# Moving rows of the MLP's output matrix onto 24 lanes, splitting its first products and single-buffering the staging tiles in a one-token attention and MLP kernel

## The chip, the cores and the metric

The kernel runs on one core of a Trainium2 chip. The metric is the device time of one execution in microseconds (us). The kernel before takes 662.61 us, the median of three runs that lie between 662.54 and 662.67.

## The reference, cut to what matters

For 4 sequences with one new token each, a normalised input feeds two branches, and the output is the input plus both.

```python
xn = _layernorm(x)                                   # x: 4 x 1 x 640
q = (xn @ wq).reshape(B, Sq, Hq, Dh)                 # 32 heads of 128
scores = einsum('bhqd,bhkd->bhqk', q, k) * Dh**-0.5  # k, v: 4 x 32 x 4096 x 128
o = einsum('bhqk,bhkd->bhqd', softmax(scores), v)
A = o.reshape(B, Sq, Hq * Dh) @ wo                   # wo: 4096 x 640

z = _gelu(xn @ w_in)                                 # w_in: 640 x 1728
z1, z2 = z[..., :864], _layernorm(z[..., 864:])
B = (z1 * (w_sp * z2 + b_sp)) @ w_out                # w_out: 864 x 640
out = x + A + B
```

The key and value caches are 134 MB each and are read once. All else that is read is about 14 MB.

## The kernel before, in words

A **unit** is one sequence and eight heads. There are 16 units (4 groups of heads, 4 sequences). A unit's keys, 8 MB, come as four quarters of 2 MB into a ring of seven places (`ring`), its values into `v_all`, 8 MB. A lane (one of 128 partitions) holds a run of 256 keys of one head.

For each quarter `n`, the loop from L688 issues `product(n)` (L504, VectorE multiplies the keys in place by the query), `fold_half(n)` (L510, VectorE adds the upper half of each key's products to the lower), `sums(n)` (L519, eight TensorE matmuls against an identity sum the rest) and, one step later, `row_sums(n)` (L532, VectorE). When a unit is complete, `head_max` and `exps` (L554, ScalarE) make the probabilities `p_c`, `by_head` (L565) spreads them to `p_m`, and `weighted` (L589, TensorE) multiplies them by the values. `take` (L601, ScalarE) copies the result to `o_rows`, `pick_unit` (L620) gathers the heads, and once per group `group_turn` and `group_proj` (L650) multiply by `wo`.

Nearly all transfers are issued on the SP queue, by `pump()`, in the order of the list `loads` (L179 to L187): half of unit 0's keys, the MLP's weights (`load_w`, L119), the other half, unit 1's keys, then values of unit u and keys of unit u+2 by turns, with `wo` after each fourth unit. A load is issued as soon as its place is free: keys when the sums that read the place are done, values when `weighted` is. Transfers in flight share eight completion semaphores, so the ninth transfer waits for the first, and so on. The instruction order on TensorE, VectorE, ScalarE and SP is the order of the program text (L684).

The MLP is the generator `gmlp()` (L362). Its parts are run between the steps of quarters 0 to 2, at the `next(mlp)` calls (L692, L701, L703, L720). The first part is the products with `w_in` (L370). The last is the products with `w_out` (L470) into the output accumulator `out_ps`. `w_in` and `w_out` lie in `v_all` until unit 0's values may be loaded.

The 864 rows of `w_out` are cut in two. Rows 0 to 767 lie on 128 lanes, six to a lane: five in `v_all` (`w_out_sb`), the sixth in `p_m` (`w_row_sb`). The last 96 rows lie on lanes 0 to 23, four to a lane, in `p_m` (`w_end_sb`). Those come by four transfers on ScalarE's queue (L117), each of six lanes (`l:FT:LS` takes every fourth lane).

At the end, the last columns of `wo` arrive in pieces, the last two of 80 KB each (L215), and the last matmuls of L650 wait for them. `out_ps` holds the two column halves of the output in lanes 0 to 3 and 32 to 35. VectorE copies the left half of these columns to `res` (L773), ScalarE the right half (L774), and two transfers write the output (L775, L776).

Of the kernel before, what the change touches and what calls it, by code (L numbers as in the profile page):

```python
# [9 lines left out]
FP32 = mybir.dt.float32  # L10
BF16 = mybir.dt.bfloat16
# [6 lines left out]
def kernel(  # L18
# [28 lines left out]
    QD = 32  # L47
# [6 lines left out]
    NR = HT * S // P  # L54
# [4 lines left out]
    RW = 8  # L59
    QW = HC * Dh  # L60
    RING = 2 * NK - 1
    NFF = Fh // P
    FR = 4
    FT = (Fh - NFF * P) // FR
    NFC = NFF + FR
    LS = 4
    NOH = D // 2
    CB = 4
    NG = NR // CB
    GW = CB * Dh  # L70
    JR = Dh // QD
# [5 lines left out]
    const = ctx.enter_context(tc.tile_pool(name="const", bufs=1))  # L77
    work = ctx.enter_context(tc.tile_pool(name="work", bufs=1))
    small = ctx.enter_context(tc.tile_pool(name="small", bufs=2))
    PSUM = bass.MemoryType.PSUM  # L80
    ps_s = ctx.enter_context(tc.tile_pool(name="ps_s", bufs=2, space=PSUM))
    ps_pv = ctx.enter_context(tc.tile_pool(name="ps_pv", bufs=2, space=PSUM))
# [12 lines left out]
    v_all = places.tile([P, NK * QW], BF16, name="v_all")  # L95
# [3 lines left out]
    w_in_sb = v_all[:, DC * HD : DC * (HD + F)].rearrange("p (c n) -> p c n", c=DC)  # L99


    NV = NFF - 1
    at_v = -(-DC * (HD + F) // 256) * 256
    w_out_sb = v_all[:, at_v : at_v + NV * D].rearrange("p (k n) -> p k n", k=NV)
    p_w = p_m[:].rearrange("p n g c h -> p (n g c h)")
    at_p = -(-D // 256) * 256
    w_row_sb = p_w[:, 0:D]
    w_end_sb = p_w[:, at_p : at_p + FR * D].rearrange("p (r n) -> p r n", r=FR)
    nc.sync.dma_start(out=wq_sb, in_=A_wq.rearrange("(p c) n -> p c n", c=DC))

    wsp_bf = const.tile([1, 1], BF16)
    bsp_bf = const.tile([1, 1], BF16)
    nc.scalar.dma_start(out=wsp_bf[:], in_=B_w_sp[0:1, 0:1])
    nc.scalar.dma_start(out=bsp_bf[:], in_=B_b_sp[0:1].rearrange("(a b) -> a b", a=1))
    w_end_rows = B_w_out[NFF * P : Fh].rearrange("(p r) n -> p r n", r=FR)
    for l in range(LS):
        nc.scalar.dma_start(out=w_end_sb[l:FT:LS], in_=w_end_rows[l:FT:LS])  # L117

    def load_w():  # L119
        nc.sync.dma_start(out=w_in_sb, in_=B_w_in.rearrange("(p c) n -> p c n", c=DC))  # L120
        w_rows = B_w_out[0 : NFF * P].rearrange("(p k) n -> p k n", k=NFF)
        nc.sync.dma_start(out=w_out_sb, in_=w_rows[:, 0:NV])
        nc.sync.dma_start(out=w_row_sb, in_=w_rows[:, NV])

    def run_of(cache, u):
        hg, b = divmod(u, Bsz)
# [122 lines left out]
    for i in range(NSTAT):  # L249
# [5 lines left out]
        out=rstd[:], in_=mv[:, 1:2], func=ACT.Sqrt, bias=eps_tile[:Bsz], scale=1.0  # L255
    )
    nc.vector.reciprocal(out=rstd[:], in_=rstd[:])
    xn_bf = work.tile([Bsz, D], BF16)
    nc.vector.tensor_scalar(
        out=xn_bf[:],  # L260
        in0=x_bf[:],
        scalar1=mv[:, 0:1],
        scalar2=rstd[:],
# [1 line left out]
        op1=ALU.mult,  # L265
    )

    xn_v = xn_bf[:].rearrange("b (p c) -> b c p", c=DC)
    xnT_ps = ps_m.tile([P, DC, Bsz], BF16, tag="m")
    for c in range(DC):  # L270
        nc.tensor.transpose(
# [2 lines left out]
    xnT = const.tile([P, DC, QD], BF16)  # L274
    nc.vector.memset(xnT[:], 0.0)
    nc.vector.tensor_copy(out=xnT[:, :, 0:Bsz], in_=xnT_ps[:])


    wq_v = wq_sb.rearrange("p c (g k e d) -> p c k e g d", g=HG, k=NQ, e=PAR)
# [59 lines left out]
    OG = 32  # L339
# [22 lines left out]
    def gmlp():  # L362
        zz, gw, gt, gz = (gm[n] for n in ("zz", "gw", "gt", "gz"))
        zT = ps_pv.tile([P, 2, NFC, Bsz], FP32, tag="pv", name="zT")
        for t in range(2):
            f1 = t * Fh + NFF * P
            w_t = w_in_sb[:, :, t * Fh : f1].rearrange("p c (f k) -> p c k f", k=NFF)
            for k in range(NFC):
                for c in range(DC):
                    nc.tensor.matmul(  # L370
                        out=zT[: P if k < NFF else FT, t, k, :],
                        lhsT=w_t[:, c, k, :]
                        if k < NFF
                        else w_in_sb[:, c, f1 + k - NFF : f1 + FT * FR : FR],
                        rhs=xnT[:, c, 0:Bsz],
                        start=(c == 0),
                        stop=(c == DC - 1),
                    )
        yield
        nc.vector.tensor_copy(out=zz[:, :, 0:NFF, :], in_=zT[:, :, 0:NFF, :])  # L380
        nc.vector.tensor_copy(out=zz[:FT, :, NFF:], in_=zT[:FT, :, NFF:])
        nc.vector.tensor_tensor(out=gw[:], in0=zz[:], in1=zz[:], op=ALU.mult)
        nc.vector.tensor_scalar(
            out=gw[:], in0=gw[:], scalar1=0.044715, scalar2=1.0, op0=ALU.mult, op1=ALU.add
# [77 lines left out]
            op=ALU.add,  # L462
        )
        nc.vector.tensor_tensor(out=gm["yT"][:], in0=gz[:, 0, :, :], in1=sq, op=ALU.mult)
        w_terms = [w_out_sb[:, k] for k in range(NV)] + [w_row_sb]
        w_terms += [w_end_sb[:FT, r] for r in range(FR)]
        for k in range(NFC):
            w = P if k < NFF else FT
            for half in range(2):
                nc.tensor.matmul(  # L470
                    out=out_sum(half),
                    lhsT=gm["yT"][:w, k, :],
                    rhs=w_terms[k][:, half * NOH : (half + 1) * NOH],
                    start=False,
                    stop=False,
                )
# [51 lines left out]
    def row_sums(n):  # L528
        u, r, t = step(n)
        if n % NK == 0:  # L530
            scores[u] = small.tile([P, NR], FP32, name="s_sb")
        nc.vector.tensor_reduce(  # L532
            out=scores[u][:, r * HC : (r + 1) * HC],
            in_=sums_ps.pop(n)[:],
            axis=AX.X,
            op=ALU.add,
        )
# [12 lines left out]

    def exps(u):
        hg, b = divmod(u, Bsz)
        p_c[u] = small.tile([P, NR], BF16, name="p_c")
        nc.scalar.activation(  # L554
            out=p_c[u][:],
            in_=scores.pop(u)[:],
            func=ACT.Exp,
            bias=maxes.pop(u)[:],
            scale=1.0,
            accum_out=row_den[hg % NACC][:, b : b + 1],  # L560
        )
# [35 lines left out]
    gr, taken, rdens = {}, {}, {}  # L597

    def take(u):
        o = taken[u] = small.tile([P, CB, Dh], FP32, name="o_rows")  # L600
        nc.scalar.copy(out=o[:].rearrange("p c d -> p (c d)"), in_=pvs.pop(u)[:])  # L601

    def group_den(hg):
# [24 lines left out]
    def group_turn(hg):  # L628
        rden = small.tile([P, 1], FP32, name="rden")
        nc.vector.reciprocal(out=rden[:], in_=rdens.pop(hg)[:])  # L630
        o_n = small.tile([P, JR, QD], BF16, name="o_n")
        nc.vector.tensor_scalar(
            out=o_n[:].rearrange("p j q -> p q j"),
            in0=gr.pop(hg)[:].rearrange("p (q j) -> p q j", j=JR),
            scalar1=rden[:, 0:1],
            scalar2=None,
            op0=ALU.mult,
        )
        o_t = small.tile([P, JR, QD], BF16, name="o_t")
        nc.vector.transpose(  # L640
            out=o_t[:].rearrange("p j q -> p (j q)"), in_=o_n[:].rearrange("p j q -> p (j q)")
        )
        gr[hg] = [
            o_t[:, j, Bsz * e : Bsz * (e + 1)] for e in range(PAR) for j in range(JR)
        ]
# [38 lines left out]
    with tc.manual_schedule(engines={E.PE, E.DVE, E.Activation, E.SP}):  # L684
# [3 lines left out]
        for n in range(NK * NU):  # L688
            u, i = divmod(n, NK)
            product(n)  # L690
            if n in (1, 2):
                next(mlp)  # L692
            if n:
                row_sums(n - 1)
            if i == 0 and u:
                head_max(u - 1)
                if waiting in taken:
                    picked(waiting)
            fold_half(n)
            if n == 1:  # L700
                next(mlp)  # L701
            if n in (1, 2):
                next(mlp)  # L703
            if i == 0 and u:
                exps(u - 1)
                if waiting in pvs:
                    take(waiting)
                by_head(u - 1)
            sums(n)
            if i == 0 and u + 1 < NU:  # L710
                stage_q(u + 1)
            if i == 0 and waiting is not None:
                if waiting in taken:
                    picked(waiting)
                if waiting % Bsz == Bsz - 1:
                    group_turn(waiting // Bsz)
                    group_proj(waiting // Bsz)
                waiting = None
            if n == 0:
                next(mlp)  # L720
            if n == 2:
                busy.remove(V)
            if n in turns:
# [45 lines left out]

        res = work.tile([P, NOH], BF16, name="res")  # L770
        out_v = out.flatten_outer_dims()
        mid = NOH // 2
        nc.vector.tensor_copy(out=res[0 : OG + Bsz, 0:mid], in_=out_ps[0 : OG + Bsz, 0:mid])  # L773
        nc.scalar.copy(out=res[0 : OG + Bsz, mid:NOH], in_=out_ps[0 : OG + Bsz, mid:NOH])  # L774
        nc.scalar.dma_start(out=out_v[:, 0:NOH], in_=res[0:Bsz])  # L775
        nc.sync.dma_start(out=out_v[:, NOH:D], in_=res[OG : OG + Bsz])  # L776

# [29 lines left out]
```

## Time and profile before

| | us |
|---|---|
| median of three runs | 662.61 |
| the profiled execution: its own time | 662.73 |
| the profiled execution: its span | 660.9 |
| VectorE busy in the span | 522.6 |
| TensorE matmul busy in the span | 311.6 |
| ScalarE busy in the span | 29.7 |

282.24 MB are read in the span, 427 GB/s. In the profile, DMA is the mean busy share of the core's 16 DMA engines. A line of the profile names the program line (L519), the engine (PE is TensorE, DVE is VectorE, ACT is ScalarE, SP is the queue that issues most transfers), and what is written and read.

The trace also holds every DMA packet: its start, duration, size and queue. It doesn't say which of the 16 DMA engines moved it. An engine moves one packet after another without a gap, so its next packet starts 3 to 6 ns before the end of the one before. That lets the packets be strung together, engine by engine, as long as no two engines are at the same point.

### The profile page before, as it was taken

The numbers are of one execution on the slowest core, as the hardware profiler recorded it, in microseconds if no ns is written. First come the engines' busy times: TensorE is split into PE (matmuls) and PEld (weight loads), VectorE is DVE, ScalarE is ACT, GpSimd is POOL, SyncE is SP. The second block draws the span as 40 slices with busy tenths as digits, with TensorE's granted clock in tenths as the row PEclk, the third lists the DMA queues.
The fourth block names the chain that finished last, engine by engine and source line by source line (L and its number), as shares of the span: only waits on it lengthen the run. The fifth ranks groups of instructions, "written<-read, shape, count | busy, mean of one in ns | idle before, by whom it ended". The sixth has DMA issues, their size and how long they took to land.

```text
span 660.9 us, 4698 instructions
## 1 busy us (share of the span) xinstructions
PE 311.6 (47%) x2035; PEld 135.9 (21%) x2035; DVE 522.6 (79%) x326; ACT 29.7 (4%) x73; POOL 2.7 (0%) x12
## 2 busy tenths in 40 slices
PE   0264363526437363462536347262452644637457
PEld 0131121212213121130222112121120221213124
DVE  2478988959597794969959597695959969999940
ACT  0020000000000000000000000000000000000000
POOL 1000000000000000000000000000000000000000
PEclk9756586766768676576767767676685767857685
DMA  9999999999999999999999999999999999999996
GB/s 374 429 449 436 418 444 440 429 440 425 436 432 437 424 437 432 440 433 424 429 445 437 424 432 433 436 433 440 428 433 432 433 436 432 414 436 428 449 412 269
DMA packets 8497, 282.56 MB, mean 428 GB/s; under 512 B 888, under 2 KB 2180, under 8 KB 3356
## 3 DMA queue, kind: packets, MB, share of 16 engines
q1 hardware_dynamic: 8408, 282.12, 99.0%
q8 instruction: 16, 0.26, 0.1%
q10 hardware_dynamic: 68, 0.13, 0.1%
q14 instruction: 5, 0.04, 0.0%
HBM read 282.24 MB, written 0.01 MB: 427 GB/s over the span
## 4 chain that ended last, share of the span: by engine, by line
DMA 60%; DVE 29%; PE 10%; issue 1%; DVEq 0%; ACT 0%
DMA k_ring<-in_A_k_cache_dram 52%; DVE k_ring L504 15%; DVE k_ring L510 8%; PE s_ps L519 7%; DMA v_all<-in_A_v_cache_dram 4%; DMA k_ring<-in_A_wo_dram 3%; DVE s_sb L532 2%; DVE p_m L565 1%; DVE m L541 1%; PE out_ps L650 1%; PE pv L589 1%; PE zT L370 1%; DVE mt L543 0%; PE out_ps L470 0%; DVE mt L546 0%
## 5 line engine op out<-in xcount | busy, mean ns | idle before, releaser
L504 DVE TENSOR_TENSOR k_ring<-k_ring,qbc 128x8192 bf16<-128x8192 bf16 x64 | 282.8, 4418 | 87.7 <-DMA k_ring<-in_A_k_cache_dram 87.7
L519 PE MATMUL s_ps<-k_ring,ident 128*128 128x512 bf16 x512 | 200.5, 562 | 313.1 <-DVE k_ring L510 313.1
L519 PEld LDWEIGHTS <-ident 128*128 128x128 bf16 x512 | 65.2, 129 | 427.1 <-issue 382.6
L510 DVE TENSOR_TENSOR k_ring<-k_ring 128x4096 bf16<-128x4096 bf16 x64 | 146.0, 2282 | 0.0
L589 PE MATMUL pv<-v_all,p_m 128*32 128x512 bf16 x960 | 60.9, 411 | 0.0
L532 DVE TENSOR_REDUCE s_sb<-s_ps 128x64 f32<-128x512 f32 x64 | 43.8, 684 | 5.5 <-PE s_ps L519 5.5
L565 DVE TENSOR_TENSOR p_m<-p_c,own 128x2048 bf16<-128x2048 bf16 x16 | 36.6, 2285 | 0.7 <-ACT p_c L554 0.7
L589 PEld LDWEIGHTS <-p_m 128*32 128x32 bf16 x992 | 26.4, 104 | 42.1 <-issue 16.7
L554 ACT ACTIVATE p_c<-s_sb,nm 128x256 bf16<-128x256 f32 x16 | 8.1, 508 | 328.8 <-DVE nm L548 328.8
L620 PEld LDWEIGHTS o_ps<-o_rows,pick 128*128 128x128 f32 x96 | 19.5, 280 | 4.3 <-issue 3.3
L620 PE MATMUL o_ps<-o_rows,pick 128*128 128x128 f32 x96 | 18.4, 356 | 0.0
L601 ACT COPY o_rows<-pv 128x512 f32<-128x512 f32 x16 | 9.4, 586 | 170.4 <-PE pv L589 170.3
L293 DVE TENSOR_SCALAR q_rows<-q_ps 128x512 bf16<-128x512 f32 x2 | 1.4, 693 | 12.5 <-PE q_ps L285 12.5
L766 DVE TENSOR_TENSOR o_n_last<-o_last,rden_all 128x32 bf16<-128x32 f32 x1 | 0.2, 192 | 13.9 <-PE o_last L758 13.9
L494 ACT CAST qbc<-qbc_ps 128x128 bf16<-128x128 f32 x16 | 4.2, 265 | 102.5 <-PE qbc_ps L486 102.5
L285 PE MATMUL q_ps<-v_all,xnT 128*32 128x512 bf16 x40 | 4.5, 630 | 8.9 <-DMA v_all<-in_A_wq_dram 8.9
L541 DVE TENSOR_REDUCE m<-s_sb 128x1 f32<-128x256 f32 x16 | 6.7, 420 | 0.6
L486 PE MATMUL qbc_ps<-q_rows,of_row 128*128 128x128 bf16 x32 | 6.1, 279 | 0.6 <-DVE q_rows L293 0.6
L486 PEld LDWEIGHTS <-of_row 128*128 128x128 bf16 x32 | 4.2, 134 | 8.2 <-issue 7.5
L667 PE MATMUL o_last<-hot,o_rows 128*128 128x8 f32 x32 | 4.9, 279 | 0.7 <-ACT o_rows L601 0.7
L667 PEld LDWEIGHTS o_last<-hot,o_rows 128*128 128x128 f32 x32 | 4.8, 226 | 1.8 <-ACT o_rows L601 1.7
L589 PE MATMUL pv<-k_ring,p_m 128*32 128x512 bf16 x32 | 3.6, 629 | 3.1 <-DMA k_ring<-in_A_v_cache_dram 3.1
(88 smaller groups left out, 73.5 us busy)
## 6 DMA issues: line engine op xcount, KB each, us to landing
k_ring<-in_A_k_cache_dram SPq DMA_DIRECT2D x6, 4096.0 KB, 15.7
v_all<-in_A_v_cache_dram SPq DMA_DIRECT2D x2, 4096.0 KB
v_all<-in_A_wq_dram SPq DMA_DIRECT2D x1, 5120.0 KB, 15.7
k_ring<-in_A_v_cache_dram SPq DMA_DIRECT2D x1, 4096.0 KB, 36.1
k_ring<-in_A_wo_dram SPq DMA_DIRECT2D x3, 1280.0 KB
v_all<-in_B_w_in_dram SPq DMA_DIRECT2D x1, 2160.0 KB, 14.8
k_ring<-in_A_v_cache_dram SPq DMA_DIRECT2D x1, 2048.0 KB
k_ring<-in_A_v_cache_dram SPq DMA_DIRECT2D x1, 1024.0 KB
```

The source lines that it names most:

```text
L486: nc.tensor.matmul(out=qb_ps[:], lhsT=of_row[:, e, b].rearrange("p k f l -> p (k f l)"), rhs=q_rows[e][:, hg, :], start=(e == 0), stop=(e ...
L504: nc.vector.tensor_tensor(out=t, in0=t, in1=qbcs[u][:, None, :].to_broadcast([P, HC, Dh]), op=ALU.mult)
L510: nc.vector.tensor_tensor(out=t[:, :, 0:HD2], in0=t[:, :, 0:HD2], in1=t[:, :, HD2:Dh], op=ALU.add)
L519: nc.tensor.matmul(out=s[:], lhsT=ident[:], rhs=t[:, :, g * RW : (g + 1) * RW], start=(g == 0), stop=(g == m - 1),)
L532: nc.vector.tensor_reduce(out=scores[u][:, r * HC : (r + 1) * HC], in_=sums_ps.pop(n)[:], axis=AX.X, op=ALU.add,)
L541: nc.vector.tensor_reduce(out=m1[:], in_=scores[u][:], axis=AX.X, op=ALU.max)
L554: nc.scalar.activation(out=p_c[u][:], in_=scores.pop(u)[:], func=ACT.Exp, bias=maxes.pop(u)[:], scale=1.0, accum_out=row_den[hg % NACC][:, ...
L565: nc.vector.tensor_tensor(out=p_m[:, u % 2], in0=p_c.pop(u)[:].rearrange("p (g c) -> p g c", c=CB)[:, :, :, None].to_broadcast([P, NG, CB, HT]
L589: nc.tensor.matmul(out=pvs[u][cg * QD : (cg + 1) * QD, :], lhsT=p_m[:, u % 2, g0 + n].rearrange("p c h -> p (c h)"), rhs=v_at[:, n * CB : ...
L601: nc.scalar.copy(out=o[:].rearrange("p c d -> p (c d)"), in_=pvs.pop(u)[:])
L620: nc.tensor.matmul(out=gr[hg][:], lhsT=pick[:, c, Bsz - 1 - b : P + Bsz - 1 - b], rhs=o[:, c, :], start=(b == 0 and c == 0), stop=(b == Bs ...
L667: nc.tensor.matmul(out=o_last[0][:, :, :, u % Bsz], lhsT=o[:, c, :], rhs=hot[:, c, :].rearrange("p (e k) -> p k e", e=PAR), start=(c == 0) ...
```

## The change

1. **Rows of `w_out`.** 512 rows (instead of 768) lie on 128 lanes, four to a lane. 112 rows lie one to a lane on lanes 0 to 111 (`w_row_sb`, now in `v_all`). 240 rows (instead of 96) lie on lanes 0 to 23, ten to a lane: six in `p_m` (`w_end_sb`), four in a new tile `w_tail`. The six come by four transfers of six lanes on ScalarE's queue, as before, but longer. The four come by four transfers of six lanes on the SP queue, issued after the queue has the second half of unit 0's keys and ahead of unit 1's. They wait until the normalised input, which borrows a row of `w_tail`, has been transposed.
2. **Terms of the MLP.** There are 15 instead of 10 blocks of rows, so 150 instead of 100 products with `w_in` and 30 instead of 20 with `w_out`, and one copy more from `zT`.
3. **Order.** `gmlp()` yields between the two halves (the one for z1, the one for z2) of its first products. The first half is issued ahead of `sums(0)`, the second after `stage_q(1)`, where both were.
4. **Buffers.** `s_sb`, `p_c`, `o_rows`, `o_n` and `o_t` have one buffer instead of two (a pool `once`).
5. **The last copy.** ScalarE copies all columns of the output in one instruction. VectorE's copy goes.

```diff
-    NFF = Fh // P
-    FR = 4
-    FT = (Fh - NFF * P) // FR
-    NFC = NFF + FR
-    LS = 4
+    NFF, FR, FT, LS = 4, 10, 24, 4
+    F0 = NFF * P
+    F1 = Fh - FR * FT
+    FX = F1 - F0
+    FA = 6
+    NFC = NFF + 1 + FR
...
+    once = ctx.enter_context(tc.tile_pool(name="once", bufs=1))
...
+    w_out_sb = v_all[:, at_v : at_v + NFF * D].rearrange("p (k n) -> p k n", k=NFF)
+    w_row_sb = v_all[:, at_v + NFF * D : at_v + (NFF + 1) * D]
+    w_end_sb = p_m[:].rearrange("p n g c h -> p (n g c h)")[:, 0 : FA * D].rearrange(
+        "p (r n) -> p r n", r=FA
+    )
+    w_tail_sb = const.tile([P, FR - FA, D], BF16, name="w_tail")
...
-    w_end_rows = B_w_out[NFF * P : Fh].rearrange("(p r) n -> p r n", r=FR)
+    w_end_rows = B_w_out[F1:Fh].rearrange("(p r) n -> p r n", r=FR)
     for l in range(LS):
-        nc.scalar.dma_start(out=w_end_sb[l:FT:LS], in_=w_end_rows[l:FT:LS])
+        nc.scalar.dma_start(out=w_end_sb[l:FT:LS], in_=w_end_rows[l:FT:LS, 0:FA])
...
-        w_rows = B_w_out[0 : NFF * P].rearrange("(p k) n -> p k n", k=NFF)
-        nc.sync.dma_start(out=w_out_sb, in_=w_rows[:, 0:NV])
-        nc.sync.dma_start(out=w_row_sb, in_=w_rows[:, NV])
+        nc.sync.dma_start(
+            out=w_out_sb, in_=B_w_out[0:F0].rearrange("(p k) n -> p k n", k=NFF)
+        )
+        nc.sync.dma_start(out=w_row_sb[:FX], in_=B_w_out[F0:F1])
...
-    xn_bf = work.tile([Bsz, D], BF16)
+    xn_bf = w_tail_sb[0:Bsz, 0, :]
...
+    for l in range(LS):
+        nc.sync.dma_start(out=w_tail_sb[l:FT:LS], in_=w_end_rows[l:FT:LS, FA:FR])
...
+            for k, w in enumerate(cols):
                 for c in range(DC):
                     nc.tensor.matmul(
...
-        yield
+            yield
...
-        nc.vector.tensor_copy(out=zz[:FT, :, NFF:], in_=zT[:FT, :, NFF:])
+        nc.vector.tensor_copy(out=zz[:FX, :, NFF], in_=zT[:FX, :, NFF])
+        nc.vector.tensor_copy(out=zz[:FT, :, NFF + 1 :], in_=zT[:FT, :, NFF + 1 :])
...
-            scores[u] = small.tile([P, NR], FP32, name="s_sb")
+            scores[u] = once.tile([P, NR], FP32, name="s_sb")
...
+            if n == 0:
+                next(mlp)
             sums(n)
...
-        mid = NOH // 2
-        nc.vector.tensor_copy(out=res[0 : OG + Bsz, 0:mid], in_=out_ps[0 : OG + Bsz, 0:mid])
-        nc.scalar.copy(out=res[0 : OG + Bsz, mid:NOH], in_=out_ps[0 : OG + Bsz, mid:NOH])
+        nc.scalar.copy(out=res[0 : OG + Bsz], in_=out_ps[0 : OG + Bsz])
```

`p_c`, `o_rows`, `o_n` and `o_t` move to `once` in the same way as `s_sb`.

More of the change, by code (lines that the diff above doesn't have):

```diff
@@ L61 @@
     RING = 2 * NK - 1
-    NFF = Fh // P
-    FR = 4
-    FT = (Fh - NFF * P) // FR
-    NFC = NFF + FR
-    LS = 4
+    NFF, FR, FT, LS = 4, 10, 24, 4
[4 more added lines that the diff above has]
+    NFC = NFF + 1 + FR
+    assert 0 < FX <= P
     NOH = D // 2
@@ L99 @@
     w_in_sb = v_all[:, DC * HD : DC * (HD + F)].rearrange("p (c n) -> p c n", c=DC)
-    NV = NFF - 1
     at_v = -(-DC * (HD + F) // 256) * 256
[L104 to L108, printed above, removed]
+    w_out_sb = v_all[:, at_v : at_v + NFF * D].rearrange("p (k n) -> p k n", k=NFF)
[4 more added lines that the diff above has]
+    w_tail_sb = const.tile([P, FR - FA, D], BF16, name="w_tail")
     nc.sync.dma_start(out=wq_sb, in_=A_wq.rearrange("(p c) n -> p c n", c=DC))
@@ L257 @@
     nc.vector.reciprocal(out=rstd[:], in_=rstd[:])
-    xn_bf = work.tile([Bsz, D], BF16)
+    xn_bf = w_tail_sb[0:Bsz, 0, :]
     nc.vector.tensor_scalar(
-        out=xn_bf[:],
+        out=xn_bf,
         in0=x_bf[:],
@@ L266 @@
     )
-    xn_v = xn_bf[:].rearrange("b (p c) -> b c p", c=DC)
+    xn_v = xn_bf.rearrange("b (p c) -> b c p", c=DC)
     xnT_ps = ps_m.tile([P, DC, Bsz], BF16, tag="m")
@@ L365, in gmlp @@
         for t in range(2):
-            f1 = t * Fh + NFF * P
-            w_t = w_in_sb[:, :, t * Fh : f1].rearrange("p c (f k) -> p c k f", k=NFF)
-            for k in range(NFC):
+            w_t = w_in_sb[:, :, t * Fh : (t + 1) * Fh]
+            cols = [w_t[:, :, 0:F0].rearrange("p c (f k) -> p c k f", k=NFF)[:, :, k] for k in range(NFF)]
+            cols.append(w_t[:, :, F0:F1])
+            cols += [w_t[:, :, F1 + r : Fh : FR] for r in range(FR)]
+            for k, w in enumerate(cols):
                 for c in range(DC):
                     nc.tensor.matmul(
[L371 to L374, printed above, removed]
+                        out=zT[: w.shape[2], t, k, :],
+                        lhsT=w[:, c],
                         rhs=xnT[:, c, 0:Bsz],
@@ L464, in gmlp @@
         nc.vector.tensor_tensor(out=gm["yT"][:], in0=gz[:, 0, :, :], in1=sq, op=ALU.mult)
[L465 to L468, printed above, removed]
+        w_terms = [w_out_sb[:, k] for k in range(NFF)] + [w_row_sb[:FX]]
+        w_terms += [w_end_sb[:FT, r] for r in range(FA)] + [w_tail_sb[:FT, r] for r in range(FR - FA)]
+        for k, w_k in enumerate(w_terms):
+            w = w_k.shape[0]
             for half in range(2):
@@ L472, in gmlp @@
                     lhsT=gm["yT"][:w, k, :],
-                    rhs=w_terms[k][:, half * NOH : (half + 1) * NOH],
+                    rhs=w_k[:, half * NOH : (half + 1) * NOH],
                     start=False,
@@ L552, in exps @@
         hg, b = divmod(u, Bsz)
-        p_c[u] = small.tile([P, NR], BF16, name="p_c")
+        p_c[u] = once.tile([P, NR], BF16, name="p_c")
         nc.scalar.activation(
@@ L599, in take @@
     def take(u):
-        o = taken[u] = small.tile([P, CB, Dh], FP32, name="o_rows")
+        o = taken[u] = once.tile([P, CB, Dh], FP32, name="o_rows")
         nc.scalar.copy(out=o[:].rearrange("p c d -> p (c d)"), in_=pvs.pop(u)[:])
@@ L630, in group_turn @@
         nc.vector.reciprocal(out=rden[:], in_=rdens.pop(hg)[:])
-        o_n = small.tile([P, JR, QD], BF16, name="o_n")
+        o_n = once.tile([P, JR, QD], BF16, name="o_n")
         nc.vector.tensor_scalar(
@@ L638, in group_turn @@
         )
-        o_t = small.tile([P, JR, QD], BF16, name="o_t")
+        o_t = once.tile([P, JR, QD], BF16, name="o_t")
         nc.vector.transpose(
```

## The prediction, as put on record

> **What bounds the kernel now.** I read the page's first, second and third parts, then the chain of waits in order of time, then the DMA packets.
>
> ```profile
> span 660.9 us, 4698 instructions
> ...
> DMA  9999999999999999999999999999999999999996
> ...
> q1 hardware_dynamic: 8408, 282.12, 99.0%
> q8 instruction: 16, 0.26, 0.1%
> q10 hardware_dynamic: 68, 0.13, 0.1%
> q14 instruction: 5, 0.04, 0.0%
> ```
>
> The 16 DMA engines are busy in every slice, and queue q1 (issued by SP) fills 99.0% of them. So the time is that of moving 282 MB, and a change counts if it alters what an engine must move, starves engines, or touches the end. The two instruction queues are small, but will matter.
>
> ```profile
> 607.66 26.88 DMA v_all<-in_A_v_cache_dram
> 634.55 21.94 DMA k_ring<-in_A_wo_dram
> 656.53 1.31 PE out_ps L650 x8
> 657.87 0.33 DVE res L773
> 658.22 0.28 ACT res L774
> ```
>
> This is the end of the chain (start, length, what): transfers up to the last pieces of wo, eight matmuls, then two copies one after the other. The last matmul record starts at 657.405; the last packet of wo is over at 657.025. The matmul ends at 657.83, VectorE starts at 657.865. So **the slowest of 16 engines sets the end.** Next to it, engines are done as early as about 653.5.
>
> I strung the packets together engine by engine. An engine never pauses once loads are queued, so its lag behind the others is a sum of what only it had to do. At 622 us the lags (us, from the earliest engine's start of unit 1's keys, packet by packet) are:
>
> ```
> engine   lag   made of
> W1       3.69  start .06, w_end .77, two fetches 2.83, small rest
> W3       3.44  start .15, w_end .77, three short fetches 2.51
> N2       3.38  start .05, late keys of unit 2 .49, two fetches 2.83
> N6       3.19  start .35, two fetches 2.85
> others   0.2 to 3.0; Nc gets 1.42 more at 648.3, so 3.19
> ```
>
> W marks the six engines that carry w_end. They are known because each of its transfers (six lanes) leaves exactly six packets of 5120 bytes on q10, one per engine, and by 46 us the same six are 0.77 later: 4 x 0.193 (0.196 less the overlap). A fetch is a 16 KB packet of q8: about 0.94 itself, and the engine's next packet takes 0.47 to 0.55 longer. The 16 of them go round eight engines in a fixed order, twice each; W1 is the only W among these. Short fetches are the five of q14 (0.31, then 0.24 to 0.53). The end agrees: W1's last packet is over at 657.025, W3's 0.23 before.
>
> **The change, part by part.** I sum against the profiled execution's own 662.73, which is 0.12 above the median.
>
> *Rows of w_out.* The durations: 5120 bytes 196 ns, 6400 bytes 244, 1280 bytes 53, so 48 ns per 1280 more; a packet of 7680 bytes is then about 292 ns (an estimate from these). Every engine loses 8 x 48 ns (w_out, 8 lanes each) and one row of w_row (7 lanes instead of 8), 0.38 + 0.05 = 0.44. The six W gain 4 x 96 ns (w_end) and 4 x 193 ns plus four semaphore packets of 6 ns (w_tail), 0.38 + 0.80. So ten engines are 0.44 earlier and **six are 0.74 later.** The trace shows no transfer of 112 lanes. Bounded by the nearest rows, it uses 16 engines as 128 lanes do (7 rows each), or six as six lanes do (19 rows, 12 x 53 = 0.64 more on the W). I take 16, because 112 is nearer to 128, and keep 0.64 for the range. The Trainium skill, "DMA: Bandwidth & Descriptors", "Why a DMA increments its semaphore by 16 and not by 1", says the largest number up to 16 that divides the lanes is used, the lowest-numbered engines first; that gives 16 for 112, and for six lanes the trace agrees with six packets. W1 is the slowest now, so the end moves by **+0.74**.
>
> *Instruction fetches.* 120 rows are added to TensorE's 3814, so fetches come a little earlier, and a seventeenth may come. By the order above it falls on the engine of the first (41.5 us), whose lag of 2.89 - 0.44 + 1.42 = 3.87 stays under W1's 4.43. Nothing.
>
> *The last copy.* VectorE's copy and the hand-over go (657.865 to 658.216); ScalarE's grows. From these rows (mean ns behind the busy time)
>
> ```profile
> L601 ACT COPY o_rows<-pv 128x512 f32<-128x512 f32 x16 | 9.4, 586 | 170.4 <-PE pv L589 170.3
> ...
> L494 ACT CAST qbc<-qbc_ps 128x128 bf16<-128x128 f32 x16 | 4.2, 265 | 102.5 <-PE qbc_ps L486 102.5
> ...
> L774 ACT CAST res<-out_ps 36x160 bf16<-36x160 f32 x1 | 0.3, 285 | 9.7 <-DVE res L773 9.7
> ```
>
> a column costs (586 - 265) / 384 = 0.84 ns, so 320 columns take 0.43. It ends at 657.88 + 0.43 = 658.31 instead of 658.50: **-0.19**.
>
> *The order of the MLP.* It is hidden as long as SP issues unit 1's keys, unit 0's values and unit 2's keys before engines run out of work. These rows set the three (start, length, what):
>
> ```profile
> 33.00 3.57 PE L519 MATMUL s_ps<-k_ring,ident 128*128 128x512 bf16 x8 [11.06 <-DVE k_ring L510]
> ...
> 36.57 4.22 PE L370 MATMUL zT<-xnT,v_all 128*128 128x4 bf16 x100
> ...
> 61.95 0.69 DVE L532 TENSOR_REDUCE s_sb<-s_ps 128x64 f32<-128x512 f32 x1 [2.20 <-PE s_ps L519]
> ...
> 76.77 0.33 SPq L148 DMA_DIRECT2D k_ring<-in_A_k_cache_dram  x1
> ```
>
> Products with 128 columns are 47 ns apart, those with 24 columns 25. A half has 25 wide and 50 narrow: 2.5 (now 30 and 20, 2.1). w_in's last packet ends at 30.90, and TensorE sees a landing 0.35 later (25.78 to 26.13 for the first keys). The first half runs 31.3 to 33.85, so `sums(0)` starts 0.85 late and SP issues unit 1's keys at 37.45, 3.6 before the first engine needs them. The second half ends at 40.0, 0.8 earlier than all do now, and VectorE's wait shrinks by as much; one copy more and 120 instead of 80 columns give back about 0.4. `out_ps` starts at 55.1 instead of 55.5, and unit 0's values go out at 56.6 instead of 57.0. But 30 products take 4.3 instead of 2.85, so `sums(2)` starts about 1.0 late, and VectorE, which waits for it at 61.95, has nothing else. Unit 2's keys go out at 77.4 to 77.8 instead of 76.77.
>
> That one is tight: of the first engines, at 80.17 to 80.2, one was held until 80.42 and its packet took 242 ns longer (N2's 0.49). With 0.6 to 1.0 more, N2 reaches 4.0 to 4.4, still not above W1's 4.43. Cost nothing, with no room to spare. A later keys issue also holds engines that lead, but those have 2 us in hand.
>
> *w_tail.* Four issues on SP, 0.68 each by the rows of w_end on ScalarE. They wait for the transposes (7.5), for w_end, and for unit 0's first keys (26.1). Behind them SP has only unit 1's keys, at 37.45. Nothing. *Single buffers.* `row_sums` of a unit must wait for `exps` of the one before. `exps` takes 0.51 while VectorE folds (2.28) and multiplies (4.42); `take` and `picked` alternate already. Nothing; without that cover 16 x 0.5 on VectorE, which waits 87.7 us for keys anyway.
>
> Sum: 662.73 + 0.74 - 0.19 = 663.28, less 0.12 for the median: **663.2**.
>
> **Rivals.**
>
> 1. *The slowest engine is none of the six.* If the fetch order starts elsewhere, W1 loses a fetch, and N2, N6 or Nc ends last. For: what the start of that order depends on is not in the trace. Against: W3 is next, with short fetches that come from other engines. From 657.02: N6 is 0.50 earlier less 0.44, so 662.61 - 0.94 - 0.19 = 661.5; with N2, 0.6 to 1.0 late, 662.7 to 663.1. About 662.3. Chance 0.18.
> 2. *Unit 2's keys come late* (slower). The place is the wait of VectorE for `sums(2)`, the price what `out_ps` and the first half really take. N2 passes W1 once SP issues later than 77.8, and each us beyond is paid in full. If narrow products with ten-column steps took twice as long (50 x 25 ns, before `sums(0)`) and the `w_out` products too (20 x 0.15), the issue comes 3 late and N2 ends 2.7 after 657.02: 662.61 + 2.7 - 0.19 = 665.1. Against: both shapes are in the trace, at 25 ns and 0.15. Chance 0.12.
> 3. *Small transfers cost a fixed time.* If w_tail's four held up q1 for their issue, 4 x 0.68 = 2.7, the time is 665.9. Against: DMA stays at 0.93 to 0.99 while w_end is issued. Chance 0.03. The Trainium skill, "DMA: Bandwidth & Descriptors", "Rules for kernel authors", advises against transfers under 64 KB as mostly overhead, which speaks against these of 30 KB; by that page's 2 us each it would be 8 us (an estimate).
> 4. *The lags don't do what I say*, and only less waiting at the end and earlier MLP work count: 661.2 or less. Chance 0.04.
>
> **How the numbers follow.** The forecast has 0.63: 663.2, between 662.8 and 663.9 (112 lanes on six engines). The range of 8 in 10 takes in most of rival 1 below and part of rival 2 above: 662.0 to 664.6. About 0.2% (1.3 us) is what a measurement of this kernel can tell from no change: 661.3 to 663.9. Faster: rival 4 and a little of rival 1, 0.06. Slower: rivals 2 and 3 and the edge of the forecast, 0.16. Same: 0.78.
>
> **What would show it.** Right: six packets of 7680 bytes per transfer on q10; the six engines 1.92 (instead of 0.77) later than the rest at 46 us and 0.7 later at the end; the last packet of wo at 657.8; ScalarE alone at the end, 0.43; unit 2's keys at 77.4 to 77.8. Wrong: an engine outside the six ends last; several engines held at 80 us; or VectorE's k_ring instructions longer than 4418 and 2282 ns, which would mean that places in memory matter.

## The result and the profile after

The changed kernel takes 664.19 us, the median of 12 executions; the kernel before, run beside it, 662.75. The ratio is 1.0022, with a 95% interval of 1.0014 to 1.0031. (One execution of the 12, 676.91, is far from the others and isn't compared.) So the time rose by 1.44 where 0.55 to 0.6 was forecast. It lies in the prediction's range of 8 in 10 (662.0 to 664.6) but outside the forecast's own band (662.8 to 663.9), and just above the 663.9 up to which the prediction would have called it no change. The profiled execution took 664.45, 1.72 more than the one before.

The page of the changed kernel, first, second and third parts (queues: packets, MB, share of 16 engines):

```profile
span 662.7 us, 4813 instructions
...
DMA  9999999999999999999999999999999999999996
...
q1 hardware_dynamic: 8440, 282.06, 98.9%
q8 instruction: 16, 0.26, 0.1%
q10 hardware_dynamic: 68, 0.19, 0.1%
q14 instruction: 5, 0.04, 0.0%
```

The DMA engines bound this kernel too; there is no seventeenth fetch. q1 has 0.06 MB less and q10 0.06 MB more, so the bytes are the same, and they fill about the same share of a longer span: packets took longer.

The end of the chain of waits (start, length, what):

```profile
609.44 26.97 DMA v_all<-in_A_v_cache_dram
636.41 0.02 issue
636.43 21.93 DMA k_ring<-in_A_wo_dram
658.36 0.04 issue
658.40 1.33 PE out_ps L660 x8
659.73 0.02 issue
659.75 0.42 ACT res L784
```

Unit 15's values take as long as before (26.97, 26.88), wo too (21.93, 21.94). They only start later. Wo's last packet is over at 658.91 instead of 657.025, so 1.89 of the loss is there at the last load. One copy instead of two gives 0.2 of it back.

The timeline of the changed kernel between 31 and 80 us has the cause:

```profile
31.29 3.56 PE L381 MATMUL zT<-xnT,v_all 128*128 128x4 bf16 x75 [9.49 <-DMA v_all<-in_B_w_in_dram]
...
34.78 3.37 PE L529 MATMUL s_ps<-k_ring,ident 128*128 128x512 bf16 x8
...
38.10 3.32 PE L381 MATMUL zT<-xnT,v_all 128*128 128x4 bf16 x75
38.19 0.35 SPq L153 DMA_DIRECT2D k_ring<-in_A_k_cache_dram  x1
...
41.53 0.19 DVE L389 COPY zz<-zT 128x32 f32<-128x32 f32 x1 [4.22 <-PE zT L381]
...
56.62 1.50 PE L480 MATMUL out_ps<-v_all,yT 128*4 128x320 bf16 x10 [2.78 <-DVE yT L474]
58.05 1.76 PE L480 MATMUL out_ps<-p_m,yT 24*4 24x320 bf16 x12
58.15 0.33 SPq L164 DMA_DIRECT2D v_all<-in_A_v_cache_dram  x1
59.60 1.27 PE L480 MATMUL out_ps<-w_tail,yT 24*4 24x320 bf16 x8
60.80 3.59 PE L529 MATMUL s_ps<-k_ring,ident 128*128 128x512 bf16 x8
64.44 0.69 DVE L542 TENSOR_REDUCE s_sb<-s_ps 128x64 f32<-128x512 f32 x1 [3.54 <-PE s_ps L529]
...
79.09 0.33 SPq L153 DMA_DIRECT2D k_ring<-in_A_k_cache_dram  x1
```

Each half of the first products takes 3.56 and 3.32 us, not 2.5. `sums(0)` starts 1.78 late (33.00 to 34.78), `out_ps` 1.1, `sums(2)` and the sums read after it 2.5 (61.95 to 64.44), and SP issues unit 2's keys at 79.09 instead of 76.77. The first engine is ready for them at 80.16. In the kernel before, four packets that start between 75 and 88 us are more than 60 ns longer than their size needs (1.3 us in all, two of the four behind a fetch). Now there are 26, together 15.9 us, or 1.0 us per engine.

To put such losses in one number I add up the bytes of all packets up to some time, take the difference to the kernel before, and divide by what 16 engines move (27.1 GB/s each: 65536 bytes in 2.418 us). This **mean lag** shows when engines waited, whichever engine it was; only what lies on six engines it hardly shows. Kernels whose loads don't differ from those of the kernel before (the last copy alone, the single buffers alone) end at -0.12 and 0.10, so a tenth means nothing. In us, from the profiled executions:

```
                     at 31   41    58    70    78    90    600
changed kernel      -0.05  0.25  0.28  0.33  0.31  1.31  1.27
after_later         -0.05  0.19  0.21  0.30  0.29  0.23  0.19
after_contig        -0.01  0.38  0.38  0.40  0.39  0.32  0.27
after_nosplit       -0.04  0.26  0.29  1.22  1.23  2.04  2.09
after_row128        -0.01  0.04  0.01  0.30  0.29  0.88  1.23
after_later_row128   0.00  0.05  0.01  0.51  0.55  0.46  0.45
before_six          -0.10 -0.09 -0.08 -0.09 -0.09 -0.12 -0.09
best                 1.65  1.67  1.68  1.67  1.68  1.59  1.58
```

The changed kernel loses 0.3 between 31 and 41 us and 1.0 around 80, and nothing after that in 500 us.

### The profile page after: what moved, and what is told of

Read it like the earlier page. It is cut to its first block, busy times and chain, and to the rows that moved or that the text cites. A ratio compares the mean times of both kernels' runs of the same rounds, so it can differ in the third digit from the quotient of the medians.

```text
span 662.7 us, 4813 instructions
## 1 busy us (share of the span) xinstructions
PE 314.3 (47%) x2095; PEld 137.8 (21%) x2095; DVE 522.7 (79%) x326; ACT 29.8 (5%) x73; POOL 2.7 (0%) x12
## 4 chain that ended last, share of the span: by engine, by line
DMA 65%; DVE 22%; PE 11%; issue 1%; ACT 0%; DVEq 0%
DMA k_ring<-in_A_k_cache_dram 48%; DVE k_ring L514 11%; DMA v_all<-in_A_v_cache_dram 9%; PE s_ps L529 8%; DVE k_ring L520 6%; DMA k_ring<-in_A_wo_dram 3%; DMA v_all<-in_A_wq_dram 2%; DMA v_all<-in_B_w_in_dram 2%; DVE s_sb L542 2%; PE zT L381 1%; PE pv L599 1%; DVE m L551 1%; PE out_ps L480 1%; PE out_ps L660 1%; DVE mt L553 0%
## 5 line engine op out<-in xcount | busy, mean ns | idle before, releaser
L514 DVE TENSOR_TENSOR k_ring<-k_ring,qbc 128x8192 bf16<-128x8192 bf16 x64 | 282.8, 4419 | 86.4 <-DMA k_ring<-in_A_k_cache_dram 86.4
L520 DVE TENSOR_TENSOR k_ring<-k_ring 128x4096 bf16<-128x4096 bf16 x64 | 146.1, 2283 | 0.0
L381 PE MATMUL zT<-xnT,v_all 128*24 128x4 bf16 (+2 forms) x150 | 6.9, 183 | 9.5 <-DMA v_all<-in_B_w_in_dram 9.5
L381 PEld LDWEIGHTS <-v_all 128*24 128x24 bf16 (+2 forms) x150 | 6.7, 134 | 10.5 <-DMA v_all<-in_B_w_in_dram 10.5
L660 PE MATMUL out_ps<-k_ring,o_t 128*4 128x320 bf16 x48 | 4.8, 355 | 0.0
```

The lines of the kernel that those rows point to most:

```text
L381: nc.tensor.matmul(out=zT[: w.shape[2], t, k, :], lhsT=w[:, c], rhs=xnT[:, c, 0:Bsz], start=(c == 0), stop=(c == DC - 1),)
L514: nc.vector.tensor_tensor(out=t, in0=t, in1=qbcs[u][:, None, :].to_broadcast([P, HC, Dh]), op=ALU.mult)
L520: nc.vector.tensor_tensor(out=t[:, :, 0:HD2], in0=t[:, :, 0:HD2], in1=t[:, :, HD2:Dh], op=ALU.add)
L660: nc.tensor.matmul(out=out_sum(half), lhsT=o, rhs=wo_sb[:, n, half * NOH : (half + 1) * NOH], start=False, stop=(hg == HG - 1 and n == HT ...
```

## The experiments

Two theories stood after the result. **Theory 1:** the mis-sized products make unit 2's keys late, and that holds all engines. **Theory 2:** the rows on six engines decide, and lags elsewhere vanish behind them. They can both hold a part. Each kernel was timed beside the kernel before (662.74 or 662.75). The intervals of the changed kernel and of most variants overlap, so a difference of 0.6 between two of them rests on the medians and on what the packets of the profiled executions show.

### The last 20 products after `sums(2)`

The 20 products with `w_out` that have 24 lanes (3 us) no longer stand ahead of `sums(2)`.

```diff
         for k, w_k in enumerate(w_terms):
+            if k == NFF + 1:
+                yield
...
             if n == 2:
+                next(mlp)
                 busy.remove(V)
```

> The changed kernel, with the last 20 products with w_out (those whose rows lie in p_m and w_tail) issued behind sums(2) instead of ahead of it. Theory 1 (unit 2's keys are issued too late, at 79.09 instead of 76.77, and all engines are held about 1.0 us at 80 to 84): sums(2) starts about 2.7 earlier, the keys go out at about 76.4, packets at 80 to 84 are no longer stretched, and the time falls by 0.8 to 1.2, to about 663.2. Theory 2 (the 0.74 more on the six engines decides): no change, 664.2.

Measured: 663.59, ratio 1.0018 (1.0008 to 1.0028). The timeline of after_later, SP's issue:

```profile
76.82 0.33 SPq L153 DMA_DIRECT2D k_ring<-in_A_k_cache_dram  x1
```

The issue is back where it was, one packet in place of 26 is held, beside a fetch, and the mean lag stays at 0.2 to 0.3. So theory 1 has 0.60 of the loss by the medians (1.03 by the last packets of the two profiled executions, 658.91 and 657.88). Of the 0.84 that is left over the kernel before, most is theory 2's: the slowest engine is 0.69 further from the mean than before (its last packet 0.86 later, the mean at the end 0.17).

### Adjacent columns

Same rows, same order; the 24 columns of `w_in` that a product reads lie side by side instead of ten apart. This part of the MLP is computed from other columns than the reference's.

```diff
-            cols += [w_t[:, :, F1 + r : Fh : FR] for r in range(FR)]
+            cols += [w_t[:, :, F1 + r * FT : F1 + (r + 1) * FT] for r in range(FR)]
```

> The changed kernel with the columns of each 24-column block of w_in taken next to each other instead of ten apart (these blocks then meet other rows of w_out than they should, so part of the MLP is computed from other columns; the amount of work is the same). Theory 1, with the column step as its cause: narrow products are 25 ns apart instead of 44, a half takes about 2.5 instead of 3.4, sums(0) starts at 33.9, unit 2's keys go out at about 77.2 to 77.6, and the time falls by about 1, to 663.2. Theory 2: 664.2. If the step is not the cause, the products stay at 44 ns.

Measured: 663.59, 1.0013 (1.0005 to 1.0022). The weight loads of these products in the changed kernel (ns: least / median / longest, then first and last start and the forms):

```profile
L381 PEld LDWEIGHTS <-v_all x150: 111/137/218, 31.3 to 41.2; 128*24 128x24 bf16 x100, 128*128 128x128 bf16 x40, 128*112 128x112 bf16 x10
```

The same in after_contig:

```profile
L381 PEld LDWEIGHTS <-v_all x150: 89/96/218, 31.4 to 39.8; 128*24 128x24 bf16 x100, 128*128 128x128 bf16 x40, 128*112 128x112 bf16 x10
```

And after_contig's timeline:

```profile
31.38 2.61 PE L381 MATMUL zT<-xnT,v_all 128*128 128x4 bf16 x75 [9.65 <-DMA v_all<-in_B_w_in_dram]
...
37.52 2.51 PE L381 MATMUL zT<-xnT,v_all 128*128 128x4 bf16 x75
37.55 0.34 SPq L153 DMA_DIRECT2D k_ring<-in_A_k_cache_dram  x1
...
56.77 0.33 SPq L164 DMA_DIRECT2D v_all<-in_A_v_cache_dram  x1
...
77.61 0.33 SPq L153 DMA_DIRECT2D k_ring<-in_A_k_cache_dram  x1
```

With the step gone a half takes the 2.5 to 2.6 of the prediction, the keys' issue falls in its 77.4 to 77.8, no packet is held there for want of the issue (one is longer, as behind a fetch), and the median falls by the same 0.60. The loads' median drops from 137 to 96 ns with count and sizes unchanged. This shows the step of the columns to be what the prediction mis-sized.

### Both halves where they were

```diff
-            if n == 0:
-                next(mlp)
             sums(n)
...
             if n == 0:
                 next(mlp)
+                next(mlp)
```

> The changed kernel with both halves of the first MLP products behind stage_q(1), as before the change (all else changed). Theory 1: sums(0) starts at 33.0 again, but the products end at 43.3 instead of 41.4, so the keys of unit 2 go out at about 81.0, 1.9 later still: 665.8; the packets of 31 to 34 us, now 0.10 to 0.19 longer, are back at 1.213, which gives back 0.26. Theory 2: 664.2, as the rows are the same.

Measured: 665.3, 1.0041 (1.0029 to 1.0053). The timeline of after_nosplit:

```profile
36.30 6.81 PE L381 MATMUL zT<-xnT,v_all 128*128 128x4 bf16 x150
...
59.85 0.33 SPq L164 DMA_DIRECT2D v_all<-in_A_v_cache_dram  x1
...
80.70 0.33 SPq L153 DMA_DIRECT2D k_ring<-in_A_k_cache_dram  x1
```

All 150 products in one piece put unit 0's values at 59.85, and there too engines come before their load: 24 packets are held by 9.5 us in all, then more at 80 us. By the medians the new order gains 1.1 on these rows, but only five executions were taken here, from 664.51 to 666.77, and the profiled one is the shortest, 0.06 above the changed kernel's. The packets of 31 to 34 us, expected back at 1.213, are not: 21 are still longer, 3.7 us in all, so it isn't the products beside them.

### Twelve lanes per transfer

Transfers of twelve lanes, so that twelve engines share what six had.

```diff
-    NFF, FR, FT, LS = 4, 10, 24, 4
+    NFF, FR, FT, LS = 4, 10, 24, 2
```

> The changed kernel with LS = 2: the 240 rows come by two and two transfers of twelve lanes, so twelve engines carry 20 rows each instead of six carrying 40. Theory 1: the keys of unit 2 are as late as before, and the time stays within 0.3 of 664.2. Theory 2: the six engines lose 20 x 0.048 = 0.95 and the time falls by 0.7 to 0.95, to about 663.3.

Measured: 664.64, 1.0029 (1.0019 to 1.0039). The fall that theory 2 wanted didn't come, but the kernel doesn't test it cleanly. With two transfers fewer on each queue SP issues `w_in` at 1.63 us instead of 16.30 (I take it that the turn of the eight shared semaphores shifts). Between 6.6 and 11.7 us 33 of wq's packets are 0.1 to 0.4 longer, 9.3 us in all, which is the mean lag of 0.53 at 25 us. More is lost near 32 and 42 us, and the lag is 1.28 at 58 us, 1.33 at the end. Unit 2's keys go out at 79.87, later still than in the changed kernel, and cost next to nothing, since the engines are late already. The slowest engine is only 0.1 to 0.2 further from the mean than before, instead of 0.69. Its last packet is over at 658.48. So the balance became better and the start worse.

### The six engines alone

On the kernel before, the four transfers of `w_end` are issued a second time, on SP (the same rows to the same place).

```diff
     pump()
+    for l in range(LS):
+        nc.sync.dma_start(out=w_end_sb[l:FT:LS], in_=w_end_rows[l:FT:LS])
```

> The kernel before, with its four transfers of w_end (six lanes, 5120 bytes a lane) issued a second time, on the SP queue, where the change issues w_tail; nothing else is changed. Theory A (the slowest engine sets the end, and it is one of the six): the six engines are 4 x 0.193 = 0.77 later, and the time rises by 0.6 to 0.8, to about 663.5. Theory B (only the mean over the engines counts): 0.12 MB over 16 engines is 0.28, so 663.0. If four more transfers on SP are what stretches packets at 31 to 34 us, that shows here too.

Measured: 663.40, 1.001 (1.0001 to 1.0019), so +0.65. The mean lag stays at -0.1 and the last packet of wo is over at 657.65 instead of 657.025. 4 x 0.193 was 0.77 on six engines of 16. No packet at 31 to 34 us is longer, so four more such transfers on SP don't stretch them. The interval of the times also holds theory B's 663.0; the last packet, 0.62 later while the mean lag stays, speaks for theory A. This tests the rule behind the prediction's first term, that the six engines decide, without the rest of the change.

### The last copy alone

On the kernel before:

```diff
-        mid = NOH // 2
-        nc.vector.tensor_copy(out=res[0 : OG + Bsz, 0:mid], in_=out_ps[0 : OG + Bsz, 0:mid])
-        nc.scalar.copy(out=res[0 : OG + Bsz, mid:NOH], in_=out_ps[0 : OG + Bsz, mid:NOH])
+        nc.scalar.copy(out=res[0 : OG + Bsz], in_=out_ps[0 : OG + Bsz])
```

> The kernel before, with the change's single last copy on ScalarE alone. By the forecast the copy takes 0.43 and ends 0.19 earlier: 662.55. If ScalarE's read of all columns cost as much as both copies did, no change.

Measured: 662.50, 0.9996 (0.9988 to 1.0005): 0.25 less, with an interval that reaches no change. The end of before_copy's chain:

```profile
656.28 1.30 PE out_ps L650 x8
657.59 0.02 issue
657.61 0.42 ACT res L772
```

Of the kernel before, the chain had 0.33 and 0.28 here, and a hand-over between them.

### Single buffers alone, order alone, and the last ten products later

Three kernels, each one edit on the kernel before. The first puts `s_sb`, `p_c`, `o_rows`, `o_n` and `o_t` in `once`, as the change does. The second has the split:

```diff
         for t in range(2):
+            if t:
+                yield
...
+            if n == 0:
+                next(mlp)
             sums(n)
```

The third puts the `w_out` products whose rows lie in `p_m` behind `sums(2)`:

```diff
+            if k == NV:
+                yield
...
+                next(mlp)
                 busy.remove(V)
```

> The kernel before with the change's single buffers for s_sb, p_c, o_rows, o_n and o_t alone. By the forecast nothing waits for them: 662.75, within 0.15. If one of the waits is late, VectorE's idle time grows and the time with it.

> The kernel before with the change's order alone: the first half of its 100 products with w_in ahead of sums(0), the rows of w_out as they were. A half has 30 products at 47 ns and 20 at 25, 2.1: sums(0) starts at about 33.4, the second half ends near 39.0 instead of 40.8, and unit 2's keys go out at about 75.0 to 75.5 instead of 76.77. No engine that ends last was held, so the time stays within 0.15 of 662.75. If the order itself costs (DMA packets stretched by the products beside VectorE's work), packets of 31 to 34 us are over 1.213 and the time rises.

> The kernel before, with the ten products of w_out whose rows lie in p_m issued behind sums(2). sums(2) starts 1.4 earlier, and unit 2's keys go out at about 75.3 instead of 76.77. Theory A (the slowest engine, W1, was not held there): within 0.15 of 662.75, though the engine held at 80.42 no longer is. Theory C (the margin at 80 us costs the kernel before something already): 0.3 to 0.5 faster.

Measured: 662.69, 662.72 and 662.72; the ratio of each is 0.9999 (0.999 to 1.0007 or 1.0008). The split brings the issue of unit 2's keys forward to 74.98, the later products to 74.78, and neither time moves: on the old rows 76.77 is early enough.

### 128 lanes instead of 112

In the changed kernel, 23 key packets at 31 to 34 us, which belong to the transfer right behind that of the 112 lanes, take 0.07 to 0.20 longer than the 1.213 they take before. Here `w_row` is loaded on all 128 lanes; the 16 more rows are not used.

```diff
-        nc.sync.dma_start(out=w_row_sb[:FX], in_=B_w_out[F0:F1])
+        nc.sync.dma_start(out=w_row_sb, in_=B_w_out[F0 : F0 + P])
```

> The changed kernel with the transfer of 112 lanes (one row each) made one of 128 lanes; the 16 rows more are loaded and not used. It asks why 24 packets of the second half of unit 0's keys take 0.07 to 0.20 longer at 31 to 34 us after the change. If the 112 lanes are the cause, the stretch goes and the time falls by about 0.25, to 663.9; if w_tail or anything else is, the stretch stays and the time is within 0.1 of 664.2.

Measured: 664.25, 1.0022 (1.0013 to 1.0032). The longer packets are gone, and the mean lag at 41 us falls from 0.25 to 0.04. The time doesn't fall, because the lag comes back where loads are issued late: to 0.30 at 70 us and 0.88 at 90. The rest of the 1.23 at the end comes between 90 and 120 us, where two dozen packets are 0.06 to 0.22 longer; why is open.

### Both repairs

after_later and after_row128 together.

> The changed kernel with both repairs: the last 20 products with w_out behind sums(2), and 128 lanes instead of 112 (16 rows more loaded, not used). With unit 2's keys early, the stretch at 31 to 34 us is no longer hidden in the wait at 80 us, so taking it away is now worth its 0.17 to 0.25: 663.4 instead of 663.59. What is left over the kernel before is then the 0.65 of the six engines less the 0.25 of the copy, 663.15 to 663.3. If the stretch doesn't count even so, 663.6.

Measured: 663.57, 1.0012 (1.0003 to 1.0021); no gain on after_later's 663.59, a miss. Its timeline:

```profile
58.45 0.33 SPq L164 DMA_DIRECT2D v_all<-in_A_v_cache_dram  x1
75.93 0.33 SPq L153 DMA_DIRECT2D k_ring<-in_A_k_cache_dram  x1
```

The keys are early now. But engines that lost nothing at 31 us are ready for unit 0's values at 60.40, 1.95 after their issue at 58.45: 15 packets between 56 and 70 us are held by 6.8 us in all, and the mean lag goes from 0.01 to 0.51. In after_later, engines 0.2 later meet the same issue (58.46) and lose 0.1. So the same late MLP has a second place where it costs, which the first loss had covered.

### An attempt at a better version

The kernel before with the single copy, the later products, and its last 96 rows on 32 lanes by four transfers of 16 lanes (two rows of a lane, then one), so that no engine carries more than another.

```diff
-    FR = 4
+    FR = 3
-    LS = 4
+    LS = 2
     for l in range(LS):
-        nc.scalar.dma_start(out=w_end_sb[l:FT:LS], in_=w_end_rows[l:FT:LS])
+        for r0, r1 in ((0, 2), (2, 3)):
+            nc.scalar.dma_start(out=w_end_sb[l:FT:LS, r0:r1], in_=w_end_rows[l:FT:LS, r0:r1])
```

> The kernel before with the single last copy, the ten p_m products behind sums(2), and the last 96 rows on 32 lanes (three a lane) by four transfers of 16 lanes, so that all 16 engines carry them evenly. By the lags: W1 and W3 lose 0.77 and gain 0.29, the other engines gain 0.29, N2 loses its 0.49 at 80 us, so the slowest (N6, Nc) is at 3.48 instead of 3.69: 0.21 earlier, and 0.25 from the copy, 662.3. If the slowest engine is not what counts, only the copy, 662.5.

Measured: 664.12, 1.0017 (1.0008 to 1.0025), single executions from 662.9 to 665.02. A miss. SP's issues in best:

```profile
2.97 0.33 SPq L149 DMA_DIRECT2D k_ring<-in_A_k_cache_dram  x1
18.11 0.33 SPq L121 DMA_DIRECT2D v_all<-in_B_w_in_dram  x1
```

`w_in` goes out 1.67 after its 16.44 of before. From 4.4 to 17 us 112 of wq's packets (40960 bytes, 1.514 before) take 0.07 to 0.39 longer, while small packets of 2560 and 1280 bytes from the rows pass; the mean lag is 1.65 by 25 us and nothing comes after. The balance itself worked: the slowest engine is no further from the mean than before. Why the large packets are slower here is open. The small size alone is not shown to be the cause: in after_spread, too, wq's packets are longer, beside packets of 7680 bytes on twelve lanes, and beside those on six lanes (the kernel before, the changed kernel) none that starts after 4 us is longer. No kernel of this study is shown to beat the one before.

## Why the prediction was right and where it was wrong

**What bounds the kernel: right.** The mean lag at the end, plus 0.65 for the six engines, less 0.25 for the copy, gives 664.42 from 662.75 for the changed kernel (its profiled execution: 664.45). For after_later it gives 663.34 (663.42), for after_contig 663.42 (663.74), for after_row128 664.38 (664.55), for after_later_row128 663.60 (663.53). So five kernels agree within 0.03 to 0.32. For after_nosplit it fails: 665.24, where the profiled execution took 664.51. There the last packet of wo is over at 658.94, 0.18 less behind the mean than in the kernel before, so the two terms don't add where many engines are held twice.

**Rows on six engines, +0.74: right.** +0.65 alone. In the five kernels that agree above, the last packet is 0.5 to 0.9 further behind the mean than in the kernel before, 0.61 in the changed kernel and 0.69 in after_later. Six packets of 7680 bytes per transfer are on q10, 291 ns each (292 forecast). That the six were 1.92 late at 46 us I could not read off, since packets held at 31 us had mixed the order; that the engine which ends last is one of the six is therefore argued from these amounts and not seen.

**112 lanes: only partly right.** They did not put 0.64 on the six engines: the slowest would be 1.38 further from the mean, and is 0.6 to 0.7. What the bounds left out is their effect on others: the keys behind them lost 0.2 to 0.3 per engine.

**The last copy, -0.19: right** (0.2 in the change, 0.25 alone; ScalarE 0.42 for 0.43). **Fetches, `w_tail`, single buffers: nothing, right** as far as the runs go: 16 fetches as before, single buffers alone 662.69; for `w_tail` before_six has four such transfers on SP, and the mean lag stays. VectorE's k_ring instructions, which the prediction named as a sign, are as long as before (4419 and 2283 ns on average). TensorE's rows on the page of before are 4070, twice 2035, where the prediction writes 3814; nothing hung on it.

**The order of the MLP: the step that failed.** "Products with 128 columns are 47 ns apart, those with 24 columns 25. A half has 25 wide and 50 narrow: 2.5." The row of 24 columns was taken for its size, though in the kernel before these columns are four apart and in the changed one ten. Spacing from one load to the next (median ns) shows it:

```
columns   step   kernel           ns
24        4      before           25
24        1      after_contig     25
24        10     changed kernel   44
128       6      before           47
128       4      changed kernel   32
112       1      changed kernel   93 (first half), 53 (second)
```

So 50 narrow products take 2.2 instead of 1.25. The 20 with 128 columns became cheaper by the same cause (step 4 for 6, 0.64 instead of 0.94), and five of 112 took about 0.4 in the first half and 0.3 in the second. The halves came to 3.56 and 3.32, the end of the second half to 41.4 instead of 40.0, `sums(2)` to 2.5 late instead of 1.0, and the keys to 79.09 instead of "77.4 to 77.8". "Cost nothing, with no room to spare" was right for 77.61, as after_contig shows, and wrong for 79.09: several engines held at 80 us was the prediction's own sign of being wrong, and it came.

**Rival 2 happened, on top of the forecast.** Its rule, each microsecond of the issue beyond 77.8 paid in full, gives 1.3 for 79.09; the changed kernel paid 1.0 in the mean lag, 0.60 in the median. Its mechanism was named in the right place (narrow products with ten-column steps), with a chance of 0.12, because "both shapes are in the trace, at 25 ns". The shape was, the step wasn't. Its other half did not come: 20 `w_out` products on 24 lanes take 3.03 us, 0.15 each, as forecast. That engines which lead "have 2 us in hand" was no cover either: at 80 us nearly all were held, and the slowest with them. That 664.19 still lies in the range is luck in part: the mechanism behind the difference was the one given 0.12, and the range covers it only through the part of that rival that it took in.

Of the 1.44, then: +0.65 rows on six engines, -0.25 the copy, +0.60 unit 2's keys. That leaves 0.44, of which the keys behind the 112 lanes would account for 0.2 (the mean lag of after_later at the end) to 0.3. That is argued from the lag and not shown by the times: taking that cause away alone gains nothing, since unit 0's values then come late. Whether the change without either, 128 lanes and adjacent columns, would reach the forecast was not tried. The rest, 0.1 to 0.2, is within what the intervals allow.

## What to carry to other kernels

Where a load-bound kernel's compute is hidden, price each issue by how long before the engines' need it comes and how many of them are there that early, place by place: taking away a loss at one place can move the need at the next one forward, as in after_later_row128. When a row's duration is borrowed for a changed instruction, compare the access pattern as well as the size, the step between elements above all. Data on a few of the 16 engines can cost nearly its whole time (here 0.65 of 0.77) if one of them ends last, however much the others have in hand, as long as no other wait has held those others back.

## What the runs showed of the hardware

- **Weight loads go by the step of the columns.** The table above: 24 columns take 25 ns at steps of 1 and 4, 44 at 10; 128 columns 32 at 4, 47 at 6. The granted clock was 0.50 in the changed kernel's first half and 0.96 in its second, and 44 and 32 ns stood in both; the kernel before had 0.50. The Trainium skill, "SBUF — State Buffer", "Door 1: The DMA port swizzle", says that reads are free up to a step of 8 two-byte elements, within lines of 16 bytes; the trace agrees for 24 columns (4 and 10) and not for 128, where 6 already costs half as much again.
- **What a late issue costs depends on how far ahead of the first engine's need it comes, and on how many engines are there.** At 3.4 us (76.77 for 80.17, before) one packet was 0.24 longer; at 2.2 (after_later, 58.46 for 60.64) 0.1 per engine was lost; at 1.95 (after_later_row128) 0.4; at 1.07 (changed kernel) 1.0. In after_spread it was 1.14 (79.87 for 81.01), but the next packets that were held start at 82.05, and three lost 1.8 us in all, 0.1 per engine.
- **Behind a transfer of 112 lanes the next packets were 6 to 16% longer** in the changed kernel (1.213 us before), 23 of them; behind one of 128 lanes (after_row128) none was. What causes it is open.
